# Attention, MLP and gated MLP in one kernel: the first attention block reordered, and its side work moved

## The chip, the cores and the metric

The kernel runs on one core of one Trainium2 chip, as one program. The metric is the device time of one execution in microseconds (us). The engines are named as the profile names them: PE is TensorE's matrix multiply, PEld its weight load, DVE is VectorE, ACT is ScalarE, POOL is GpSimd, SP is SyncE, which here only issues DMAs. "PEq", "SPq" and so on are the instruction queues of these engines.

## What is computed

Three layers follow one another: decayed causal attention, a normalised MLP with a residual, and a second MLP whose gate mixes the positions of a sequence.

```python
# attention: B=4, H=8, S=576, D=64
scores = (1/sqrt(D)) * q @ k.T
cum    = cumsum(log(clip(f, 1e-4, 1)))
scores = where(causal, -1e9, scores + cum[:, None] - cum[None, :])
x      = softmax(scores) @ v                      # heads side by side: 512 wide
# first MLP, 512 -> 2048 -> 512
xn = (x - mean(x)) / sqrt(var(x) + 1e-6) * g_ln
x  = x + relu(xn @ w_ch1) @ w_ch2
# second MLP
h  = relu(x @ w_in); u, v = h[:, :512], h[:, 512:]
vs = einsum("ts,bsd->btd", w_spatial, norm(v)) + b_spatial
out = (u * vs) @ w_out
```

## The kernel before

The 2304 positions are cut into nine blocks of 256 columns (the list `BLOCKS`, line 43). A block holds two batches times 128 queries, or one batch times 256 queries; blocks 0 and 1 are the first 128 positions of batches 0, 1 and of batches 2, 3. `attention32` (L324) computes these two in float32, four pairs of heads each; `attention1` computes blocks 2 and 3, and `attention` the rest. For each pair `attention32` does four score matmuls (L356; the decay comes in as two extra rows of the operands, 64 and 65), mask and row minimum on DVE (L359), the exponential with its sum on ACT (L361), 1/sum (L364, L365), a diagonal matrix of 1/sum on DVE (L369), four matmuls that transpose and scale (L373), a copy out of PSUM on ACT (L374, the tile `PT`), four matmuls with v (L381) and a copy of the result into `xT` on ACT (L382). In L381 the second head of a pair uses 128 columns of v and writes all 128 rows of PSUM, then the first head uses 64 columns and overwrites the upper half.

When the four pairs of a block are there, `norm` (L614) makes the mean over the 512 channels (L622, L611), subtracts it (L625, "centre"), squares (L628), adds on POOL (L632, L633), makes the mean of the squares (L611), and from it 1/sqrt, the tile `y` (L636 to L640). For the first block `y` is not applied to the input of the MLP; it is applied at the very end of the group (L738), since relu lets a positive factor through.

The first MLP runs over eight groups of blocks; group 0 is block 0, group 1 is block 1. A group walks over 16 slices j of the hidden width: `ph(j)` is x times a slice of w_ch1 (L708, 8 instructions in float32), a relu on ACT (L715), and two steps later `acc` gets the slice of w_ch2 (L693). The weights come in as 64-bit floats, 1 MB for a slice: `load_raw` (L539) issues the DMAs, `narrow` (L518) makes 32-bit floats of them with two passes on ACT (L531, L532) and three on DVE (L533 to L535). `PACE` and `LOWAT` (L58, L59) say behind which event the ACT passes of the first slices may stand; the marks are `done[i]` (i counts PT copies of block 0, then relus) and "split" (the last copy of the scaled input of group 0, L672). Group 0 runs in float32 while the weights arrive. `squares(j)` (L561) multiplies each weight slice with itself on PE (L569) to get the weights' norms; `scales` (L575) sums them and derives power-of-two scales (the matmul L588 is the mark "sums"); `make16(j)` (L593) then splits each slice into two 16-bit halves in place (ACT L598, DVE L601). Groups 1 to 7 run on these halves. `SUMS = 13` keeps ph(13) and what is behind it in group 0 back until "sums", as work for PE during the change from group 0 to group 1. `vnorm` (L228) does the same as `squares` for v: five loads of 1 MB and 80 matmuls (L246), needed by block 3 and later.

At the start `decays` (L146) computes the cumulative logarithm on DVE and ACT; the decay rows of block 0 go from SBUF to SBUF by DMA (L343). `gscale` (L188) loads the norm's weights g_ln broadcast over 128 partitions and derives a scale; it is used from group 1 on. `WARM = 54` dummy matmuls (L1039) run on PE while the first loads arrive.

The program text gives each step a place on a common time line (`SPAN`, `BEGIN`, `CONV`, `MAKE`, `VN`, L48 to L62, and the list of events in `run`). A planner then orders the instructions of each engine by this order and by its own estimate of when each is ready; `after` (L123) adds an order between two instructions without a semaphore. Each engine and each DMA queue works its list strictly in that order. Pools of SBUF tiles have a fixed number of buffers (`BUFS0` for blocks 0 and 1), and a PSUM bank has a tag: `acc` and `ph` have two banks, `s2` two, `s` and `av` one each.

## Time and profile before

| | us |
|---|---|
| median of 3 runs | 790.46 (790.35 to 790.98) |
| the profiled execution | 790.74 |
| its span, first to last instruction | 789.0 |
| PE busy | 765.5 (97%) |
| DVE busy | 549.5 (70%) |
| ACT busy | 520.5 (66%) |
| POOL busy | 60.3 (8%) |
| mean granted TensorE clock | 0.989 |

A busy time on PE is the time between the start of a matmul and its modelled end; dummy matmuls count, and so do matmuls at half clock. The page's slices show where PE is idle or slow; the table of windows gives PE, DVE, ACT and the granted clock of any stretch; the list of waits says for whom an engine waited; the timeline gives the instructions in the order of time. Seven eighths of the span are groups 1 to 7 and the second MLP, which the change does not touch.

### The profile page before, as it was taken

How to read it: one execution, taken by the hardware profiler on the slowest of the kernel's cores; microseconds unless marked ns; L12 is line 12 of the kernel's file. 1: busy time of each engine (PE TensorE's matmuls, PEld its weight loads, DVE VectorE, ACT ScalarE, POOL GpSimd, SP SyncE). 2: the span in 40 equal slices, each digit the busy share in tenths (PEclk: the TensorE clock that was granted, in tenths of full speed). 3: DMA queues.
4: the chain of work that ended last, by engine and by line, in shares of the span. 5: the costliest groups of instructions: out<-in, count | busy, mean ns of one | idle time of the engine just before them, and what ended most of it. 6: DMA issues, size and time to landing. Idle time of an engine off the chain costs nothing.

```text
span 789.0 us, 16305 instructions
## 1 busy us (share of the span) xinstructions
PE 765.5 (97%) x5978; PEld 581.9 (74%) x5978; DVE 549.5 (70%) x1490; ACT 520.5 (66%) x1315; POOL 60.3 (8%) x89
## 2 busy tenths in 40 slices
PE   8799999999999999999999999999998999999998
PEld 7488887887877877788888888544446667668676
DVE  5699589849389889979858855687526662654634
ACT  5787489839388889888858844485417633656543
POOL 4100011011011001110201100100021000000000
PEclk8989999999999999999999999999999999999999
DMA  8888576278679998996995955731043230000101
GB/s 255 220 305 292 188 210 104 55 145 125 142 208 165 189 242 151 204 220 140 195 186 120 125 88 172 198 111 50 1 78 50 80 109 1 31 31 7 57 1 61
DMA packets 164228, 104.72 MB, mean 133 GB/s; under 512 B 106179, under 2 KB 151363, under 8 KB 164149
## 3 DMA queue, kind: packets, MB, share of 16 engines
q1 hardware_dynamic: 157848, 96.63, 50.9%
q0 software_dynamic: 5296, 5.28, 5.3%
q10 hardware_dynamic: 1004, 1.78, 0.8%
q8 instruction: 47, 0.77, 0.4%
q14 instruction: 33, 0.26, 0.1%
HBM read 64.37 MB, written 15.11 MB: 101 GB/s over the span
## 4 chain that ended last, share of the span: by engine, by line
PE 58%; DVE 13%; issue 12%; ACT 7%; DMA 7%; POOL 1%; SPq 1%; DVEq 0%; ACTq 0%; POOLq 0%
PE ph L708 13%; PE acc L693 12%; PE pb L648 7%; PE pb L649 7%; PE pb L650 7%; PE av L460 3%; PE s L296 3%; DVE P L317 2%; DMA PT<-P 2%; DVE wt L601 2%; DMA vr<-in_v_dram 2%; DMA qk<-in_qk_dram 1%; DVE sd L300 1%; PE gram L569 1%; PE av L381 1%
## 5 line engine op out<-in xcount | busy, mean ns | idle before, releaser
L693 PE MATMUL acc<-hh,wt 128*128 128x256 f16 (+2 forms) x960 | 198.5, 296 | 0.8 <-DVE t L736 0.5
L708 PE MATMUL ph<-xh,wt 128*128 128x256 f16 (+1 forms) x896 | 187.3, 289 | 5.6 <-DVE hl L719 5.2
L708 PEld LDWEIGHTS <-wt 128*128 128x128 f16 x1344 | 127.1, 98 | 52.0 <-issue 13.7
L693 PEld LDWEIGHTS <-wt 128*128 128x128 f16 x1344 | 129.2, 98 | 44.1 <-issue 5.2
L708 PE MATMUL ph<-xl,wt 128*128 128x256 f16 (+1 forms) x448 | 129.3, 289 | 0.0
L693 PE MATMUL acc<-hl,wt 128*128 128x256 f16 (+1 forms) x416 | 115.9, 282 | 0.3 <-DVE hl L719 0.3
L715 ACT ACTIVATE hh<-ph 128x256 f16<-128x256 f32 (+2 forms) x128 | 51.0, 399 | 60.4 <-PE ph L708 60.2
L719 DVE SCALAR_TENSOR_TENSOR hl<-ph,hh 128x256 f16<-128x256 f32 (+1 forms) x112 | 50.5, 453 | 40.1 <-ACT hh L715 39.6
L261 ACT ACTIVATE P<-sd,st 128x512 f16<-128x512 f32 (+1 forms) x128 | 70.5, 586 | 9.6 <-DVE st L307 7.9
L317 DVE SCALAR_TENSOR_TENSOR P<-sd,st,P 128x384 f16<-128x384 f32 (+1 forms) x96 | 58.6, 633 | 9.3 <-ACT P L261 8.8
L304 ACT ACTIVATE sd<-sd,st 128x384 f32<-128x384 f32 (+2 forms) x80 | 54.6, 683 | 15.2 <-DVE st L300 15.0
L296 PE MATMUL s<-x 68*128 68x384 f32 (+7 forms) x256 | 63.3, 360 | 0.1
L300 DVE CUSTOM_DVE_ANT_0 sd<-s,mask 128x384 f32<-128x384 f32 (+2 forms) x80 | 45.8, 579 | 3.9 <-PE s L296 2.8
L740 POOL DMA_DIRECT2D x_d<-t x36 | 32.3, 1081 | 188.4 <-DVE t L736 149.3
L261 ACT ACTIVATE x<-qk 64x320 fp32r<-64x320 f32 (+1 forms) x64 | 41.4, 699 | 1.0 <-DMA qk<-in_qk_dram 1.0
L991 DVE SCALAR_TENSOR_TENSOR u<-pb,wsc,u 128x288 f32<-128x288 f32 x32 | 15.9, 514 | 34.3 <-PE pb L990 34.3
L296 PEld LDWEIGHTS s<-x 68*128 68x128 f32 (+3 forms) x256 | 36.9, 178 | 2.4 <-issue 0.9
L648 PE MATMUL pb<-wsh,vl 128*128 128x288 f16 x128 | 36.6, 286 | 1.3 <-ACT u L934 1.1
L649 PE MATMUL pb<-x2l,wih 128*128 128x288 f16 (+2 forms) x144 | 37.8, 273 | 0.0
L648 PE MATMUL pb<-x2h,wil 128*128 128x288 f16 (+2 forms) x144 | 37.8, 273 | 0.0
L650 PE MATMUL pb<-x2h,wih 128*128 128x288 f16 (+2 forms) x144 | 37.8, 273 | 0.0
L650 PE MATMUL pb<-wsh,vh 128*128 128x288 f16 x128 | 36.6, 286 | 0.0
(281 smaller groups left out, 1596.8 us busy)
## 6 DMA issues: line engine op xcount, KB each, us to landing
raw<-in_moe_w_ch_dram SPq DMA_DIRECT2D x32, 512.0 KB
qk<-in_qk_dram SPq DMA_DIRECT2D x32, 448.0 KB
vraw<-in_v_dram SPq DMA_DIRECT2D x5, 1024.0 KB
vr<-in_v_dram SPq DMA_DIRECT2D x16, 320.0 KB
x_d<-xT SPq DMA_DIRECT2D x9, 512.0 KB
x_d<-t POOLq DMA_DIRECT2D x36, 128.0 KB, 4.4
out_dram<-o SPq DMA_DIRECT2D x32, 144.0 KB
raw<-in_moe_w_in_dram SPq DMA_DIRECT2D x8, 512.0 KB
```

Source lines behind the costliest of these rows:

```text
L261: self.nc.scalar.activation(out, in_, AF.Copy, scale=scale)
L296: nc.tensor.matmul(ps[: R * u + R, : c1 - c0], lhsT=x[:, lo - q0 - R * u : hi - q0], rhs=y[:, c0:c1], start=g == 0, stop=g == len(heads[u] ...
L300: nc.vector.tensor_tensor_reduce(out=sd[:M, c0:c1], in0=ps[:M, : c1 - c0], in1=mask, scale=-0.125, scalar=3e38 if n == 0 else st[:M, n - 1 ...
L304: nc.scalar.activation(sd[:M, :N], sd[:M, :N], AF.Exp, bias=st[:M, n : n + 1], scale=-1.0, accum_out=st[:M, 2:3])
L317: low = nc.vector.scalar_tensor_tensor(out=dl, in0=src, scalar=rs, in1=dh, op0=ALU.mult, op1=ALU.subtract)
L648: first = mm(out, lhsT=al, rhs=bh, start=start, stop=False, **kw)
L649: mm(out, lhsT=ah, rhs=bl, start=False, stop=False, **kw)
L650: mm(out, lhsT=ah, rhs=bh, start=False, stop=stop, **kw)
L693: ins = nc.tensor.matmul(acc[m], lhsT=a, rhs=b, start=bank not in clear, stop=last and e == len(terms) - 1, skip_group_check=True)
L708: ins = nc.tensor.matmul(ph, lhsT=a, rhs=b, start=k == e == 0, stop=k == NK - 1 and e == len(terms) - 1)
L715: relu = nc.scalar.activation(hh, ph, AF.Relu)
L719: nc.vector.scalar_tensor_tensor(out=hl, in0=ph, scalar=0.0, in1=hh, op0=ALU.max, op1=ALU.subtract)
```

## The change

- **Block 0 only: all scores first.** The four pairs' scores, minimum, exponential and 1/sum come ahead of all transposes and products with v. The tile `e` gets a fourth buffer; the scores of pairs 2 and 3 go to the `s2` banks.
- **Fills.** `WARM` falls from 54 to 34 dummy matmuls; new dummy matmuls of the same kind (`fill`, 256 columns in bf16) stand behind the scores of pairs 1 and 3 (4 each), behind the transposes of each pair (4) and behind its products with v (3): 36 in all.
- **Loads of block 0.** The two decay rows are issued from two queues, SP and ACT, behind two pairs of q and k; v comes behind all four pairs. Both DMAs of the first weight slice now stand behind these loads (before, only the first of the two did).
- **v zero-padded.** `vm` holds v of each head with zeros in the other head's 64 columns. Two memsets on DVE and, for each block, two copies on POOL. The products with v now all have 128 columns, and the second head adds to the first.
- **Work moved from ACT and POOL in `decays`.** The negated decay rows go from ACT to POOL, two memsets from POOL to DVE.
- **Deferred.** The second step of block 0's norm (from L628 on) and `gscale` come at 0.1 of group 0, `gscale` on POOL's DMA queue and behind "split". Two copies on ACT into `mask4` come behind "split".
- **First weights earlier.** The first ACT pass of slice 1 stands behind "x3", the copy L382 of pair 3, and no longer behind "split"; its DVE passes stand behind "centre". The second ACT pass of slices 1 and 2 stands behind "x3" and "split".
- **Squares, scales, vnorm.** `squares(j)` stands behind ph(j) (from slice 9 on one slice ahead); the sums are taken behind ph(14), and `SUMS` is 15, so that only ph(15) is kept back. The matmuls of `vnorm` stand behind ph(0) of group 1. Block 1's first scores stand behind the first squares.

```diff
-BUFS0 = dict(vr=1, qk=1, e=3, diag=2, PT=2, st=4)
+BUFS0 = dict(vr=1, qk=1, e=4, diag=2, PT=2, st=4)
-WARM = 54
+WARM, FILLS = 34, (4, 4, 3)
-PACE = (1, "split", "split", "split", "split")
-LOWAT = (1, 2, 3)
-SUMS = 13
+PACE = (1, "x3", "split", "split", "split")
+LOWAT = (1, "x3", "split")
+SUMS = 15
+REST = 0.1
+BESIDE = 9
-WSC, MAKE, VN = 0.63, 0.64, 0.7
+WSC, MAKE, VN = 0.875, 0.876, 1.01
...
+        for e, t, r, w in ((nc.gpsimd, decay, 1, P), (nc.vector, f32(dec), 2, S), (nc.gpsimd, dec1, 1, P)):
+            e.memset(t[:, :r, w:], 1.0)
+            e.memset(t[:, r:, :w], 1.0)
...
-        nc.scalar.activation(dec[:, 2, S:], f32(h), AF.Copy, scale=-1.0)
-        nc.scalar.activation(dec[:, 3, S:], f32(l), AF.Copy, scale=-1.0)
+        for r, x in ((2, h), (3, l)):
+            nc.gpsimd.tensor_scalar(out=dec[:, r, S:], in0=f32(x), scalar1=-1.0, scalar2=1.0, op0=ALU.mult, op1=ALU.mult)
...
-        nc.scalar.dma_start(out=g, in_=self.moe_g_ln.rearrange("p k -> (p k)").partition_broadcast(P))
+        nc.gpsimd.dma_start(out=g, in_=self.moe_g_ln.rearrange("p k -> (p k)").partition_broadcast(P))
...
+    def fill(self, n, behind=None):
+        ones = self.ones.bitcast(BF16)
+        for i in range(n):
+            ins = self.nc.tensor.matmul(self.warm[:, : 2 * P], lhsT=ones[:, :P], rhs=ones, start=True, stop=True)
+            if behind is not None:
+                self.after(ins, behind)
+                behind = None
...
+        if not b:
+            self.vm = at.tile([P, 2, NP, 2, P], F32, name="vm")
+            for u in range(2):
+                clear = nc.vector.memset(self.vm[:, :, :, u, 64 - 64 * u : P - 64 * u], 0.0)
+                self.after(clear, self.scan)
...
-                    loads.append(nc.sync.dma_start(out=row, in_=self.decay[b * H : (b + 2) * H, r]))
-                loads.append(nc.sync.dma_start(out=vra, in_=self.v[b : b + 2, :P].rearrange("b p d -> p b d")))
+                    queue = nc.scalar if r and not b else nc.sync
+                    loads.append(queue.dma_start(out=row, in_=self.decay[b * H : (b + 2) * H, r]))
+        loads.append(nc.sync.dma_start(out=vra, in_=self.v[b : b + 2, :P].rearrange("b p d -> p b d")))
+        for u in range(2):
+            us = slice(64 * u, 64 * u + 64)
+            v = vra.rearrange("p n (q w) -> p n q w", w=P)
+            nc.gpsimd.tensor_copy(out=vm[:, :, :, u, us], in_=v[:, :, :, us])
...
+            elif p == 0:
+                for i in range(NP):
+                    ahead.append(scores(i))
+                    yield
...
-            for n in range(2):
-
-                for u in (1, 0):
-                    mm(pav[: 64 * u + 64, 0, n], lhsT=vr[:, n, : 64 * u + 64], rhs=pt[:, n, u], start=True, stop=True, skip_group_check=True)
+            for n, u, c in four_:
+                ins = mm(pav[:, 0, n], lhsT=vm[:, n, p, u], rhs=pt[:, n, u], start=u == 0, stop=u == 1, skip_group_check=True)
...
-        nc.sync.dma_start(out=raw[:, DM:], in_=self.moe_w_ch2[cs, :])
+        second = nc.sync.dma_start(out=raw[:, DM:], in_=self.moe_w_ch2[cs, :])
+        if j == 0:
+            self.after(second, self.marks["loads"])
...
+            if g == 0:
+                self.marks["hidden"] = ins
+                if j < BESIDE:
+                    self.squares(j)
+                if BESIDE <= j + 1 < NF:
+                    self.squares(j + 1)
...
+            if n == 0:
+                with self.tc.high_priority(1):
+                    next(g)
+                self.rest = g
+                return xc
```

## Rows read from the trace of the kernel before

**Rows 1.** Windows: from:to, length, busy us (instructions) by engine, granted clock, DMA share, GB/s.

```profile
14.00:21.00 7.00, 6.97 (x31) 6.16 (x29) 4.16 (x22) 4.95 (x26) 0.00 (x0) 0.51 1.07 384
...
34.00:38.00 4.00, 2.35 (x9) 1.08 (x7) 1.41 (x2) 4.00 (x6) 2.00 (x2) 0.98 0.44 144
38.00:45.00 7.00, 5.88 (x22) 4.89 (x22) 6.60 (x9) 6.66 (x18) 0.00 (x0) 0.52 0.91 315
45.00:100.00 55.00, 55.00 (x366) 47.38 (x365) 42.86 (x75) 35.24 (x67) 0.00 (x0) 1.00 0.71 250
```

**Rows 2.** Waits of PE, 0 to 62 us: for whom, total us, times, longest.

```profile
PE gram L569 <- DVE wt L535: 1.1, 1, 1.1
```

**Rows 3.** Timeline to 34 us: start, length, engine, line, operation, count, idle before.

```profile
0.81 0.92 SPq L154 DMA_DIRECT2D ft<-in_f_dram  x1
...
3.19 0.61 SPq L546 DMA_DIRECT2D raw<-in_moe_w_ch_dram  x1
3.57 0.52 DVE L168 TENSOR_SCALAR ft<-ft 32x128 f32<-32x128 f32 x2 [2.35 <-DMA ft<-in_f_dram]
...
5.26 1.23 SPq L343 DMA_DIRECT2D qk<-decay  x2
...
10.14 2.05 PE L356 MATMUL acc<-qk 66*128 66x128 f32 x16
...
13.17 3.39 PE L356 MATMUL acc<-qk 66*128 66x128 f32 x16 [0.98 <-DMA qk<-in_qk_dram]
...
30.45 0.38 ACT L382 ACTIVATE xT<-s 128x256 f32<-128x256 f32 x1 [0.71 <-PE s L381]
...
33.40 1.56 PE L708 MATMUL ph<-xg,wt 128*128 128x256 f32 x6 [1.25 <-ACT xg L672]
```

**Rows 4.** Chain of waits, 0 to 140 us: start, us, engine, line, instructions.

```profile
67.42 0.46 PE gram L569 x8
...
69.66 1.36 PE av L381 x8
...
76.14 1.73 PE ph L708 x8
...
80.53 0.89 PE s L373 x8
```

**Rows 5.** Lines 361, 374 and 531 to 100 us: ns min/median/max, starts.

```profile
L361 ACT ACTIVATE e<-e,st x32: 385/388/422, 11.8 to 84.1; 128x128 f32<-128x128 f32 x32
...
L374 ACT ACTIVATE PT<-ph x4: 575/597/599, 18.6 to 28.1; 128x512 f32<-128x512 f32 x4
...
L531 ACT ACTIVATE wt<-raw x16: 1118/1149/1173, 21.5 to 89.9; 128x1024 f32<-128x1024 f32 x16
```

**Rows 6.** Lines 693 and 708, from the sums to group 1: ns, starts.

```profile
L693 PE MATMUL acc<-hh,wt x45: 379/379/462, 100.5 to 124.1; 128*128 128x256 f32 x45
...
L708 PE MATMUL ph<-xg,wt x24: 379/379/462, 101.8 to 116.5; 128*128 128x256 f32 x24
```

**Rows 7.** Timeline of the change from group 0 to group 1.

```profile
100.75 0.28 PE L588 MATMUL gram<-gss,ones 128*128 128x2 f32 x2
...
119.67 1.71 ACT L669 ACTIVATE xh<-xT,gs 128x256 f16<-128x256 f32 x4 [1.47 <-DVE xT L642]
...
125.26 0.27 PE L708 MATMUL ph<-xh,wt 128*128 128x256 f16 x1
```

**Rows 8.** Windows around the start of group 1, columns as above.

```profile
101.00:125.00 24.00, 24.00 (x179) 20.98 (x179) 22.21 (x65) 20.63 (x53) 2.39 (x3) 1.00 0.82 199
...
130.00:137.00 7.00, 5.79 (x31) 4.03 (x31) 7.00 (x25) 7.00 (x19) 0.00 (x0) 0.76 0.35 82
```

**Rows 9.** Timeline, 108 to 112 us: DVE and POOL side by side.

```profile
108.24 0.75 DVE L601 SCALAR_TENSOR_TENSOR wt<-wt,w2c 128x512 f16<-128x512 f32 x1
...
108.95 1.27 POOL L632 TENSOR_TENSOR sq<-sq 128x512 f32<-128x512 f32 x1 [71.70 <-ACT sq L628]
...
109.66 1.12 DVE L601 SCALAR_TENSOR_TENSOR wt<-wt,w1c 128x512 f16<-128x512 f32 x1
```

More of the change, by code (lines that the diff above doesn't have):

```diff
@@ L349, in attention32, with scores @@
         yield
-        for p in range(NP):
-            qk, vr = qka[:, p], vra[:, :, p * P : (p + 1) * P]
-            ps, e, diag = bank(tags[0]), four("e"), four("diag")
+        def scores(p):
+            qk = qka[:, p]
+            ps, e = bank("s2" if p > 1 else tags[0]), four("e")
             st = at.tile([P, 2, 4], F32, tag="st", name="st", bufs=bufs["st"])
-            four_ = [(n, u, 2 * n + u) for n in range(2) for u in range(2)]
             for n, u, c in four_:
-                mm(ps[:, n, u], lhsT=qk[:, u, n, :P], rhs=qk[:, u, n, P:], start=True, stop=True, skip_group_check=True)
+                ins = mm(ps[:, n, u], lhsT=qk[:, u, n, :P], rhs=qk[:, u, n, P:], start=True, stop=True, skip_group_check=True)
+                if b and p == c == 0:
+                    self.after(ins, self.first)
+            if not b and p % 2:
+                self.fill(FILLS[0], ins)
             for n, u, c in four_:
@@ L365, in attention32 @@
             nc.vector.reciprocal(st[:, 1], st[:, 1])
[L366 to L368 removed]
+            return e, st
+        four_ = [(n, u, 2 * n + u) for n in range(2) for u in range(2)]
+        ahead = []
+        for p in range(NP):
+            if b:
+                ahead.append(scores(p))
+                yield
+            elif p == 0:
+                for i in range(NP):
+                    ahead.append(scores(i))
+                    yield
+            e, st = ahead[p]
+            ps, pt, diag = bank(tags[1]), four("PT"), four("diag")
             nc.vector.tensor_tensor(
@@ L515, in tail, with narrow @@
         return d[:, c : c + n].rearrange("(k p) t -> p k t", p=P)
-    def narrow(self, raw, tmp, low=None):
+    def narrow(self, raw, tmp, low=None, behind=None):
         nc = self.nc
@@ L558, in load_w @@
         if j < len(LOWAT):
-            self.after(self.low, self.done[LOWAT[j]])
+            self.after(self.low, self.marks[LOWAT[j]] if isinstance(LOWAT[j], str) else self.done[LOWAT[j]])
     def squares(self, j):
@@ L1036, in run @@
         self.at = at_cm.__enter__()
-        warm, ones = self.bank("s2"), self.ones.bitcast(BF16)
-        for i in range(WARM):
-            self.nc.tensor.matmul(warm[:, : 2 * P], lhsT=ones[:, :P], rhs=ones, start=True, stop=True)
+        self.warm = self.bank("s")
+        self.fill(WARM)
         with self.pool("dk") as dk:
@@ L1123, in run @@
             elif kind == -1:
-                if n < NF:
+                if n < 0:
+                    drain(self.rest)
+                    self.gscale()
+                elif n < NF:
                     self.load_w(n)
                     converted = n + 1
-                    if n >= len(CONV):
-                        for i in range(n + 1) if n == len(CONV) else [n]:
-                            self.squares(i)
                 elif n == NF:
```

50 lines of the change are left out of this document (30 added, 20 removed).

## The prediction

> **What bounds the kernel now.** I first read the windows, to see where PE is idle or slow, since PE is busy for 97% of the span and the rest of the kernel cannot move unless PE's work starts earlier or gets less. From 45 to 100 us PE is busy in all of the 55 us at the full clock, while DVE is busy for 42.9 and ACT for 35.2 us [rows 1]: here PE is the bound, and the other two have slack of 12 and 20 us. The front is different. The first MLP matmul stands at 33.40 us [rows 3]; PE's work before it is the attention of block 0, which is a chain, and dummies. After it PE is idle for 1.65 us from 34 to 38 and for 1.12 us from 38 to 45, and from 38 to 45 it has about half the clock (1.2 instead of 2.4 GHz), so that 5.88 us of busy time do about 3.0 us of full-speed work [rows 1]. So the front loses 33.4 us to the chain and then 2.8 + 2.9 = 5.7 us. The second place is the start of group 1 at 125.26 us [rows 7]: from 130 to 137 PE is idle for 1.2 us and has a granted clock of 0.76, which costs 7 x 0.24 = 1.7 us, while DVE and ACT are busy all the time [rows 8]. These two places are what the change touches; everything behind them I take as PE-bound and moved as a whole.
>
> Next I read the timeline of the front. The decay rows are issued at 5.26 us, as the cumulative sum is ready, and the first scores run at 10.14 us; the scores of pairs 2 and 3 wait for q and k until 13.17 us; the last result of block 0 is copied from 30.45 to 30.83 us [rows 3].
>
> **The change, step by step.** The sum goes against the profiled execution: 790.74 us, of which the span is 789.0; the median of the runs is 0.28 us lower, which I leave out of account.
>
> *First scores.* A DMA into an empty queue, that of f, takes from 0.81 to 3.57 us, 2.76 us from issue to landing; the decay rows take from 5.26 to 10.14 us, 4.88 us, though they are small, as 512 KB of raw weights were issued at 3.19 us ahead of them, with g_ln's broadcast [rows 3]. Both move behind. By the 2.76 us the first scores stand at 8.0 us: 2.1 us earlier. The second row on ACT's queue saves one of two issues, half of 1.23 us [rows 3], which is in these 2.1. Bounds: 0.6 (only that issue) to 2.7. Moved past SP's queue is v: it lands behind all four pairs, and its first reader is the product of pair 0, which waits for a PT copy anyway. The two DVE memsets fit into the 2.35 us in which DVE waits for f [rows 3].
>
> *Body of block 0.* From the first scores to the last copy it takes 30.83 - 10.14 = 20.7 us [rows 3]. New: ACT begins 1.7 us after the first scores, as now (11.8, [rows 5], against 10.14), at 9.7 us. Sixteen exponentials at 0.39 us [rows 5] take 6.2 us and the four small copies between them at most as much as one each, to 16 to 17.5 us; PT copies cannot go earlier, if the planner keeps to program order. I take 16.4. By then PE has done all scores and two transposes. What is left is a chain of PT copy (0.6 us, [rows 5]), transposes, PT copy, products, copy, on PE four times the products, twice the transposes, at 0.89 us per four matmuls [rows 4] = 5.3 us, some 17 fills ahead of the last product, and the last copy of 0.38 us [rows 3]. A fill lies between an instruction of the transposes, 0.89 / 8 = 0.11 us, and one of ph, 1.73 / 8 = 0.22 us [rows 4]; nearer to the first, as it is one pass in 16 bits: 17 x 0.11 = 1.9 us. With 0.9 us for the steps between the engines: 16.4 + 0.6 + 5.3 + 1.9 + 0.4 + 0.9 = 25.5 us for the end of the last copy, a body of 17.5 us: a gain of 3.2. Bounds: 5.2 (fills and transposes hide behind ACT) and -0.2 (a stretch at half clock like that from 14 to 21 us, clock 0.51 [rows 1], which costs 7 x 0.49 = 3.4 us, comes back, though the fills are there).
>
> *From the last copy to the MLP.* 30.83 to 33.40 us, 2.6 us of sum, mean, subtraction and scaling [rows 3], is unchanged in itself: the first MLP matmul stands at 28.1 us. The wait for "x3" now lets two ACT passes of slice 1 start, 1.15 us each [rows 5]; behind them on ACT stand the scaled inputs, ready some 2 us after "x3", so that they may come 0.3 us late. That is part of the next bound.
>
> *The gap behind it.* PE waits there for slice 1, which DVE narrows late (1.1 us, [rows 2]), as its ACT pass stands behind "split", and for the squares and means of the norm. The ACT pass now stands behind "x3", 2.6 us earlier, and the norm's second step is gone to 0.1 of the group, where DVE and ACT have slack. I leave about 1.3 us of idle time and 1.7 us for half a stretch at low clock, as PE still has holes between the last product and slice 1: 3.0 instead of 5.7, a gain of 2.7. Bounds: 0.5 (the low clock stays in full and only the norm's mean drops out) to 4.7 (1 us is left).
>
> *Products with v.* Four matmuls with 128 and 64 columns in turn take 1.36 us, those of the transposes, as many and as large, 0.89 us [rows 4]. With 128 columns throughout I price them at 0.89. In block 1, which runs where PE is full, this gives 4 x 0.47 = 1.9 us; block 0's share is in its body. Bounds: 0 to 1.9, as no row shows the padded form; the transposes are nearest in shape and type. The POOL copies of v lie beside the exponentials; behind them on POOL stands nothing that block 0 reads, and the products wait for them.
>
> *POOL's copies against DVE.* A POOL addition of 512 columns takes 1.27 us, and the DVE instruction beside it 1.12 us instead of 0.75 [rows 9]. Two copies in block 0 may meet the diagonals on DVE: 0.4 us, bounds 0 to 1.5. The Trainium skill ("SBUF — State Buffer", "Who interferes with whom") says that a DVE instruction with two SBUF inputs and a GpSimd one that reads SBUF exclude each other for the whole instruction. By that rule two copies would cost up to 2.5 us, and the sum would be 2.1 us higher; the row shows a stretch of 0.37 us, not of 1.27.
>
> *Squares and the handover to group 1.* The squares cost PE the same wherever they stand. But the sums now follow ph(14). In the old order 45 + 24 instructions of group 0 are behind the sums [rows 6], which at 1.73 us for 8 [rows 4] are 14.9 us; now ph(15) and three steps of `acc` are, 32 instructions, 6.9 us. And the 80 matmuls of `vnorm`, as large as those of the squares (0.46 us for 8, [rows 4]), 4.6 us, go behind group 1's ph(0). So PE has 12.6 us less to fill the handover, which took 100.75 to 125.26 us, 24.5 us [rows 7]. What must happen in it is less than that: the sums, the scales and one `make16` (about 3 us), and the scaled input of block 1, made at 119.67 us [rows 7] behind five `make16` and block 2's first steps on full DVE and ACT queues (22.2 and 20.6 of 24 us, [rows 8]). Block 1 itself ends earlier with the front, and in the new order the sums come later relative to it, so its norm can go first. I price the handover at no change: its cover is 6.9 us of group 0 and the scores of block 2. Bounds: -2.9 (the idle and low-clock time behind 130 us goes) to +3.
>
> *At nothing.* The deferred `gscale`, the copies into `mask4` and the negated decay rows on POOL lie beside PE's full stretch or are read much later, by block 2 on; if the cover were gone, these ten short instructions, at no more than an exponential's 0.39 us [rows 5], would cost up to 3.9 us.
>
> Sum: 2.1 + 3.2 + 2.7 + 1.9 - 0.4 = 9.5 us; 790.7 - 9.5 = **781.2 us**.
>
> **The rivals.**
>
> *PE paces block 0.* Scores, transposes and products at 0.89 to 1.0 us each make 11 us, 36 fills 4 us or more: nearly as much as the body itself. With one stretch at half clock it grows by 3.4 us: 784.6. For it: the clock fell at 14 us after PE had waited for 0.98 us [rows 3], and 20 fewer warming matmuls leave a hole before the scores.
>
> *The new order does not come out.* The planner places each instruction by its own estimate; if the narrowing of slice 0 or late exponentials stand between the PT copies, the body keeps its 20.7 us and 2.1 + 2.7 + 1.9 - 0.4 = 6.3 us are left: 784.4, and with the gap at its lower bound 786.6. I take 785.5.
>
> *The handover is freed.* If DVE and ACT have worked off block 2's first steps before the sums, the 2.9 us go too: 778.3.
>
> *POOL excludes DVE.* If a diagonal waits for a whole copy, two copies of 1.27 us [rows 9] stand in the way instead of 0.4 us: 783.3. This is the rule quoted above.
>
> *Slower: the handover starves PE.* The front hands 9.5 us to group 0, but 14.9 - 6.9 = 8.0 us more of group 0 stand ahead of the sums, so these come at about 99.3 us, 1.5 us earlier only. If DVE and ACT still need 24.5 us from there, group 1 starts at 123.8 us, PE has stood idle for a good 10 us, the 4.6 us of `vnorm` follow on PE's path, and a low clock after the idle time costs another 1.7 us: -1.5 + 4.6 + 1.7 = +4.8, 795.5 us. It ends slower from a handover of 20 us on. Against it: block 1 ends earlier, and most of the 22.2 us of DVE are not needed for group 1's first step.
>
> **How the numbers follow.** The forecast has 0.50, PE pacing block 0 0.15, the order not coming out 0.12, the freed handover 0.08, POOL's exclusion 0.05, the starved handover 0.10. The range of 8 in 10 takes in the unknown costs of the front, of which the bounds won't all fall on one side, and all rivals but the slower one: 775.5 to 788.0. A measurement can tell 0.2%, 1.6 us, from no change. Slower by that: 0.09; within: 0.04, from the worst ends of the second and the slower rival; faster: 0.87.
>
> **What would show it.** The first scores at about 8 us; sixteen exponentials in one run on ACT; the copy of pair 3 at about 25 us; the first MLP matmul at about 28 us, and less than 1.5 us of idle time behind it; 0.9 us for the products of a pair; the sums near 99 us and group 1's first matmul by 110 us. Wrong would be: a last copy later than 28 us, a clock of 0.5 after 28 us for as long as before, or PE idle by several us between the sums and group 1.

## The result and the profile after

The changed kernel takes 800.5 us (median of 4 runs, 798.2 to 803.4) against 790.4 us for the kernel before (790.2 to 791.0) on the same chip: a ratio of 1.013, 95% interval 1.009 to 1.016. It is slower by 10 us where 781.2 us was predicted. The profiled execution took 801.2 us with a span of 799.5 us, 10.5 us more than that of before (789.0).

I read the two traces by four marks that every kernel here has: the first MLP matmul of group 0, the first matmul of group 1 (`ph` of 16-bit halves), and the moments at which POOL issues the first store `x_d` of each group. The differences between marks say in which stretch time is won or lost:

| stretch, us | before | after | difference |
|---|---|---|---|
| start to first MLP matmul | 33.40 | 29.98 | -3.4 |
| to group 1's first matmul | 91.86 | 93.71 | +1.9 |
| to group 1's store | 68.87 | 73.77 | +4.9 |
| to group 2's store | 56.57 | 57.24 | +0.7 |
| to group 4's store | 131.73 | 137.60 | +5.9 |
| to the end of the span | 406.57 | 407.20 | +0.6 |

The stores of groups 1, 2 and 4 (start, length, engine, line, operation, count, idle before), first of the kernel before, then of after:

```profile
194.13 2.67 POOL L740 DMA_DIRECT2D x_d<-t  x3 [18.84 <-DVE t L736]
...
250.70 2.69 POOL L740 DMA_DIRECT2D x_d<-t  x3 [7.34 <-DVE st L307]
...
382.43 2.68 POOL L740 DMA_DIRECT2D x_d<-t  x3 [5.50 <-DVE t L736]
```

```profile
197.46 2.63 POOL L798 DMA_DIRECT2D x_d<-t  x3 [21.64 <-DVE t L794]
...
254.70 2.65 POOL L798 DMA_DIRECT2D x_d<-t  x3 [9.52 <-DVE t L794]
...
392.30 2.67 POOL L798 DMA_DIRECT2D x_d<-t  x3 [6.64 <-DVE t L794]
```

The front wins 3.4 us. Up to group 1's store twice as much (6.8 us) is lost again, and another 5.9 us are lost between the stores of groups 2 and 4 (254.7 to 392.3 us), in whose program text nothing was changed.

The timeline of the front after (start, length, engine, line, operation, count, idle before):

```profile
2.74 0.74 POOL L196 DMA_DIRECT2D gall<-in_moe_g_ln_dram  x1
...
5.18 0.59 SPq L362 DMA_DIRECT2D qk<-decay  x1
...
9.09 2.02 PE L379 MATMUL acc<-qk 66*128 66x128 f32 x16 [2.01 <-DMA qk<-decay]
...
10.71 0.40 ACT L388 ACTIVATE e<-e,st 128x128 f32<-128x128 f32 x1 [3.59 <-DVE st L386]
...
16.68 0.39 ACT L388 ACTIVATE e<-e,st 128x128 f32<-128x128 f32 x1
...
27.12 0.38 ACT L423 ACTIVATE xT<-s 128x256 f32<-128x256 f32 x1 [1.27 <-PE s L420]
...
29.98 1.99 PE L758 MATMUL ph<-xg,wt 128*128 128x256 f32 x8 [1.27 <-ACT xg L722]
...
34.71 1.56 PE L758 MATMUL ph<-xg,wt 128*128 128x256 f32 x6 [1.32 <-DVE wt L577]
```

Beside [rows 3]: the first scores stand at 9.09 us instead of 10.14, all sixteen exponentials run without a break from 10.71 us on, the last copy ends at 27.50 instead of 30.83, and the gap behind the first MLP matmul is down to the wait of 1.32 us for DVE. The front does what the change says but for one load: g_ln's broadcast (`gall`) is still issued at 2.74 us, ahead of the decay rows. Only its use is deferred, not the load, though the description of the change and the forecast have both behind. Windows after (columns as in rows 1), to be read beside [rows 1] and [rows 8]:

```profile
14.00:21.00 7.00, 5.66 (x36) 5.36 (x37) 3.61 (x12) 5.47 (x22) 0.00 (x0) 0.76 1.04 386
34.00:38.00 4.00, 3.29 (x21) 2.89 (x22) 4.00 (x13) 3.88 (x10) 3.18 (x2) 1.00 0.71 253
38.00:45.00 7.00, 6.73 (x37) 5.57 (x36) 6.61 (x12) 5.66 (x14) 0.00 (x0) 1.00 0.80 249
60.00:80.00 20.00, 18.34 (x125) 16.25 (x124) 17.66 (x29) 15.09 (x26) 0.00 (x0) 1.00 0.86 294
100.00:120.00 20.00, 14.76 (x86) 12.72 (x84) 16.19 (x57) 16.64 (x46) 2.14 (x2) 0.95 0.36 93
120.00:140.00 20.00, 14.26 (x101) 10.57 (x102) 17.62 (x49) 17.76 (x44) 3.58 (x4) 0.71 0.51 92
```

The same two last windows of the kernel before:

```profile
100.00:120.00 20.00, 20.00 (x140) 17.48 (x140) 17.21 (x52) 16.01 (x41) 2.33 (x2) 1.00 0.82 226
120.00:140.00 20.00, 18.79 (x158) 15.22 (x159) 20.00 (x57) 19.84 (x51) 3.58 (x4) 0.91 0.59 91
```

From 100 to 140 us PE was busy for 38.8 of 40 us; now it is busy for 29.0, and from 120 on with a mean granted clock of 0.71. What PE waited for, 98 to 150 us (engine, line, waited for, total us, times, longest), and its timeline in that place:

```profile
PE av L474 <- DMA PT<-P: 3.8, 2, 3.2
PE av L474 <- DVE t L688: 2.9, 1, 2.9
PE ph L758 <- ACT xh L719: 1.8, 1, 1.8
```

```profile
107.02 0.28 PE L637 MATMUL gram<-gss,ones 128*128 128x2 f32 x2
107.16 1.97 PE L758 MATMUL ph<-xg,wt 128*128 128x256 f32 x8
...
111.54 1.99 PE L743 MATMUL acc<-hh,wt 128*128 128x256 f32 x8 [0.77 <-ACT hh L773]
...
117.33 0.53 PE L474 MATMUL av<-PT,vp 128*64 128x128 f16 x12 [2.93 <-DVE t L688]
...
123.69 0.58 PE L758 MATMUL ph<-xh,wt 128*128 128x256 f16 x2 [1.80 <-ACT xh L719]
```

The sums (107.02) come 6.3 us later than before [rows 7], and behind them PE has 16 matmuls of group 0 left, ph(15) and one step of `acc`, and after 113.5 us only block 2 and waits until group 1 begins at 123.69 us. Before, the matmuls of `vnorm` lay there as well. Windows of `vnorm`'s instructions alone (length, busy us and count of PE, PEld and DVE, clock, DMA share, GB/s), first of the kernel before, then of after:

```profile
100.00:120.00 20.00, 4.22 (x57) 0.00 (x0) 0.00 (x0) 1.00 0.82 226
120.00:140.00 20.00, 1.97 (x26) 0.30 (x2) 0.83 (x2) 0.91 0.59 91
```

```profile
150.00:160.00 10.00, 1.88 (x31) 0.00 (x0) 0.00 (x0) 1.00 0.46 89
160.00:170.00 10.00, 2.92 (x43) 0.00 (x0) 0.00 (x0) 1.00 0.97 277
170.00:180.00 10.00, 0.92 (x14) 0.30 (x2) 0.85 (x2) 1.00 0.58 157
```

`vnorm` filled 6.2 us of the handover; now it has none there, and its 5.7 us stand between 150 and 180 us, where PE is full anyway (busy for 29.5 of 30 us).

### The profile page after: what moved, and what is told of

Its sections match the earlier page's. It is cut to its first block, busy times and chain, and to the rows that moved or that the text cites. A ratio compares the mean times of both kernels' runs of the same rounds, so it can differ in the third digit from the quotient of the medians.

```text
span 799.5 us, 16351 instructions
## 1 busy us (share of the span) xinstructions
PE 759.0 (95%) x5994; PEld 581.8 (73%) x5994; DVE 553.9 (69%) x1494; ACT 521.8 (65%) x1313; POOL 63.6 (8%) x94
## 4 chain that ended last, share of the span: by engine, by line
PE 59%; DVE 12%; issue 12%; DMA 9%; ACT 7%; POOL 1%; SPq 0%; ACTq 0%; DVEq 0%; POOLq 0%
PE acc L743 13%; PE ph L758 12%; PE pb L698 7%; PE pb L699 7%; PE pb L700 7%; PE s L299 4%; PE av L502 3%; DMA PT<-P 3%; DMA raw<-in_moe_w_ch_dram 2%; DVE P L320 1%; DMA vr<-in_v_dram 1%; ACT x L264 1%; DMA vraw<-in_v_dram 1%; DVE low L576 1%; ACT sd L307 1%
## 5 line engine op out<-in xcount | busy, mean ns | idle before, releaser
L758 PEld LDWEIGHTS <-wt 128*128 128x128 f16 x1344 | 128.1, 99 | 52.8 <-issue 14.7
L299 PE MATMUL s<-x 68*128 68x384 f32 (+7 forms) x256 | 61.7, 357 | 2.0 <-DVE x L282 0.8
```

What stands on the lines that cost most here:

```text
L299: nc.tensor.matmul(ps[: R * u + R, : c1 - c0], lhsT=x[:, lo - q0 - R * u : hi - q0], rhs=y[:, c0:c1], start=g == 0, stop=g == len(heads[u] ...
L758: ins = nc.tensor.matmul(ph, lhsT=a, rhs=b, start=k == e == 0, stop=k == NK - 1 and e == len(terms) - 1)
```

## The experiments

Single executions of these runs spread by some 4 us to either side (the kernel before: 787 to 796), so whole times are given with the interval of their ratio. Each kernel has one trace, so a stretch of a single kernel shows little by itself, and stretches are compared over several kernels. Two theories: **A**, the handover from group 0 to group 1 costs the 10 us that the front doesn't; **B**, part of the loss is that the planner orders the untouched later groups differently (against it A', that the later loss hangs on the handover too). The planned lists of SP's queue bear on B: from block 4 on they are the same, entry by entry, in the changed kernel and in the front-only kernel, and the same in the kernel before and in that with the handover alone (run 2). I call these two the order of after and the order of before.

**1. The front alone.** The changed kernel with the old handover; the squares are back at the events that load the weights, and the order of vnorm behind ph(0) is out. The change also draws the events of the five `make16` and of `vnorm` closer together (steps of 0.001 and 0.015 instead of 0.02 and 0.05); this run takes that back too, and run 2 has it.

```diff
-SUMS = 15
+SUMS = 13
-WSC, MAKE, VN = 0.875, 0.876, 1.01
+WSC, MAKE, VN = 0.63, 0.64, 0.7
...
-                    self.after(ins, self.marks["entered"])
```

> The changed kernel with the handover of before: the sums behind ph(13), scales and make16 at 0.63 and 0.64 of group 0, the norm's sums of w (vnorm) from 0.7 on, the squares where they were. The new front stays: all scores first, the decay rows on two queues, zero-padded v, the deferred second step. Theory A (the handover costs some 8 us, and the later stretch from 325 to 392 us some 8 us more, which belongs to the new front, since the queue order of SP's transposes and loads in the later groups is that of the changed kernel here too): first x_d store of group 0 about 120, of group 1 about 189, of group 3 about 318, of group 4 about 385, and 790 to 793 us in all. Theory A' (all of the loss hangs on the handover, the later stretch too): 785 us, with group 4 stored at about 377. If the front itself is what costs, group 0's store stands no earlier than 123 and the time is 795 or more.

791.8 us, ratio 1.003 (1.001 to 1.006). Group 0 is stored at 118.33 us, group 1 at 188.08: 6.1 us earlier than before, while group 4 (382.50) is where it was. As A foretold, but for group 3, stored at 313.55 and not at about 318; A' is out.

**2. The handover alone**, on the kernel before, with vnorm behind group 1's ph(0) and squares(j) behind ph(j).

```diff
-SUMS = 13
+SUMS = 15
+BESIDE = 9
-WSC, MAKE, VN = 0.63, 0.64, 0.7
+WSC, MAKE, VN = 0.875, 0.876, 1.01
...
+                    self.after(ins, self.marks["entered"])
```

> The kernel before, with the new handover alone: sums behind ph(15), squares behind ph, scales and make16 at 0.875, vnorm behind group 1's ph(0). Front and products with v as before. Theory A: from group 0's x_d store (124.9) to group 1's it takes 77.4 us as in the changed kernel, and not 69.2, so +8 at group 1; the queue order of the later groups is that of before, so nothing more is lost after it: 798 us. Theory A' (the later loss belongs to the handover): 806 us. If the handover costs only because the front ended early: no change, 790 to 791 us.

799.4 us, ratio 1.013 (1.011 to 1.015): the handover alone is as slow as the whole change. Group 1 is stored at 202.55, 8.4 us later than before; the sums stand at 110.95. From 95 to 105 us DVE and ACT have next to nothing to do, where in the front-only kernel they are full. First this kernel, then the front-only one:

```profile
95.00:105.00 10.00, 10.00 (x60) 8.28 (x59) 0.70 (x2) 0.80 (x3) 0.00 (x0) 1.00 0.34 99
```

```profile
95.00:105.00 10.00, 10.00 (x72) 8.81 (x71) 9.77 (x20) 9.70 (x24) 1.52 (x2) 1.00 0.81 240
```

**3. make16 of slices 1 to 4 later.** Those of the slices behind them move back by four places as well.

```diff
-SOON = 5
+SOON = 1
```

> The changed kernel, but make16 of slices 1 to 4 comes in group 1's first half and not ahead of its first scaled input. Theory C (the handover is long because make16 and block 2's steps stand ahead of block 1's norm on DVE and ACT): group 1's first ph 3 to 5 us earlier than 123.7, and the time 3 us or more below the changed kernel's 800.5. Theory D (the sums come too late, and PE has no work left to cover the norm, whoever stands ahead): within 1.5 us of 800.5.

796.4 us, ratio 1.007 (1.003 to 1.011). Group 1's first matmul stands at 115.13 us, 8.6 earlier than in the changed kernel (1.3 of them from the start of the MLP), and group 1's store 5.9 earlier. So the five `make16` ahead of block 1's scaled input do delay it once the sums are late (with early sums this was not tried); group 1 itself then takes longer (76.4 us to its store).

**4. vnorm early again, sums late.**

```diff
-WSC, MAKE, VN = 0.875, 0.876, 1.01
+WSC, MAKE, VN = 0.875, 0.876, 0.89
...
-                    self.after(ins, self.marks["entered"])
```

> The changed kernel, but the 80 matmuls of vnorm may run as soon as the scales are made, ahead of group 1's ph(0), where PE waits. If vnorm costs its 4.6 us on PE's path behind ph(0): 796 us. If the wait of PE for the transposes of block 2 and for the norm sets the end anyway, or vnorm's operands are late too: within 1.5 us of 800.5.

805.6 us, ratio 1.020 (1.016 to 1.023): both expectations missed, it got worse. The last two loads of v go out as late as 113.8 and 114.8 us, and PE now waits for loads of v in the middle of the handover (98 to 150 us):

```profile
PE vgram L248 <- DMA vraw<-in_v_dram: 4.2, 2, 3.0
```

Group 1's first matmul stands at 129.50 us, and its store comes 78.1 us later, though `vnorm` no longer stands in that stretch (changed kernel: 73.8). With late sums, then, vnorm does better behind ph(0); that is no gain against early sums.

**5. One dummy more before the kernel.** Nothing but this, on the kernel before:

```diff
-WARM = 54
+WARM = 55
```

> The kernel before with one dummy matmul more in its warming run (55 instead of 54), nothing else. Theory B: what costs 7 to 9 us between the stores of groups 3 and 4 is the order that the planner gives to the later groups, and it depends on the smallest shift of the front; with this one matmul SP's queue of the later groups comes out in the order of the changed kernel. Then the interval from group 3's x_d store to group 4's is 67 to 69 us and not 59, and the time 797 to 799. If the front's work itself (other data in flight, the deferred second step) causes the later loss: 790.5 to 791 us.

798.0 us, ratio 1.006 (1.003 to 1.008). The interval from group 3's store to group 4's is 67.15 us, as B foretold, but group 2 to 3 takes 3.8 us less than before, so that the two together cost 4.2 us; another 2.4 us are lost ahead of group 1's store.

**6. The front alone, one fill more in each place**, which brings the order of before back:

```diff
-WARM, FILLS = 34, (4, 4, 3)
+WARM, FILLS = 34, (5, 5, 4)
```

> The front-only kernel with one more fill matmul in each place (5, 5, 4 instead of 4, 4, 3). More work by 11 dummies, but SP's queue of the later groups comes out in the order of before. Theory B: groups 3 to 4 take 59 to 60 us again, and the front's gain of 6 to 9 us stays to the end: 782 to 784 us. Otherwise as the front-only kernel: 791 to 793.

790.6 us, ratio 0.998 (0.996 to 1.001). Group 3 to 4 takes 60.3 us, as expected; but group 2 to 3 takes 75.2 instead of 69.6, and the gain is not there at the end. The expected 782 to 784 us were missed.

**7. The changed kernel with 3 fills each**, the order of before again:

```diff
-WARM, FILLS = 34, (4, 4, 3)
+WARM, FILLS = 34, (3, 3, 3)
```

> The changed kernel with 3, 3, 3 fills instead of 4, 4, 3; its later queue order is that of before. Theory B with A: the later loss goes, the handover's 8 us stay: group 0 to 1 takes 77 us, group 3 to 4 60 us, 792 to 794 us in all. If the later loss hangs on the handover: 800.

793.7 us, ratio 1.002 (0.999 to 1.004). Group 0 to 1 takes 77.9 us, group 3 to 4 60.2 us, as expected: the handover's loss stays and the later one shrinks, without any change to the handover. Six fills less (one behind the transposes of each pair, one behind the scores of pairs 1 and 3) bring the ratio from 1.013 to 1.002.

**8. vnorm behind group 1's ph(0), sums early**, on the kernel before:

```diff
-WSC, MAKE, VN = 0.63, 0.64, 0.7
+WSC, MAKE, VN = 0.63, 0.64, 1.01
...
+                    self.after(ins, self.marks["entered"])
```

> The kernel before, but vnorm's 80 matmuls stand behind group 1's ph(0); sums, scales and make16 as before (sums behind ph(13)). If the missing cover of vnorm's 4.6 us and their place on PE's path is what makes the handover long: group 0's store to group 1's 4 to 5 us longer than the 69.2 of before. If the late sums are (scales and block 2 wait for them, and DVE and ACT idle until then): within 1.5 us of 69.2. The order of the later groups is a third one here, so the whole time says little.

791.5 us, ratio 0.999 (0.996 to 1.002). Group 0 to 1 takes 74.4 us, 5.2 more than before, about the 4 to 5 of the first case. Group 1's first matmul comes at 121.0 us, 4.2 earlier than before, and its store 3.7 later. Another, shorter order of the later groups (130.5 us from group 2 to 4) gives that back.

**9. The front alone with fills 2, 2, 2**, yet another order:

```diff
-WARM, FILLS = 34, (4, 4, 3)
+WARM, FILLS = 34, (2, 2, 2)
```

> The front-only kernel (new front, old handover) with fills 2, 2, 2 instead of 4, 4, 3. SP's queue in the later groups is a third order, neither that of before nor that of the changed kernel. Theory B (the order decides): from group 1's store to the end not the 600.2 us of the front-only kernel but another figure, which I can't foretell; group 1's store at 188 to 190. If fills matter for the front, group 0's store lies 2 us or more later than the 118.3 of the front-only kernel, with a lower clock in block 0.

785.5 us, ratio 0.994 (0.992 to 0.996): faster than the kernel before and than the changed one. Group 1 is stored at 184.76, earlier than I had expected, group 2 to 4 takes 130.5 us. The clock is at 0.50 from 14 to 21 us (run 1: 1.00) and the first MLP matmul stands at 32.01 us, 1.6 us later than in run 1; group 0's store lies 1.1 us later, not 2 or more.

**10. Sums two steps earlier, vnorm still late.**

```diff
-SUMS = 15
+SUMS = 13
-WSC, MAKE, VN = 0.875, 0.876, 1.01
+WSC, MAKE, VN = 0.70, 0.701, 1.01
...
-                if j < BESIDE:
-                    self.squares(j)
-                if BESIDE <= j + 1 < NF:
-                    self.squares(j + 1)
+                for i in [j] if j < 8 else [2 * j - 8, 2 * j - 7]:
+                    if i < NF:
+                        self.squares(i)
```

> The changed kernel with the squares of two slices per step from ph(8) on, so that the sums stand behind ph(12) and not behind ph(14); the scales and make16 follow at 0.70. vnorm stays behind group 1's ph(0). Theory A1 (the lateness of the sums keeps DVE and ACT idle until 107 us, and leaves PE too little of group 0): DVE and ACT are busier before 105 us, group 1's store at 192 to 194 and not 197.5, 3 to 5 us earlier. Theory A2 (all that counts is vnorm behind ph(0)): group 1's store within 1.5 us of 197.5. The later groups have another order here, so it's read from group 1's store.

792.7 us, ratio 1.004 (1.002 to 1.006). The sums come at 92.31 us, 14.7 us earlier than in the changed kernel and earlier even than before. Group 1's first matmul comes 3.8 us and its store 4.7 us earlier than in the changed kernel (1.2 of them from the start of the MLP): A1's figure. A good half of the handover's loss stays with the late vnorm.

**11. The front alone without fills**, the order of before:

```diff
-WARM, FILLS = 34, (4, 4, 3)
+WARM, FILLS = 34, (0, 0, 0)
```

> The front-only kernel without any fills; SP's queue in the later groups is that of before. If the fills hold the clock up in block 0: from 14 to 28 us the granted clock is lower than in the front-only kernel (as in the kernel before, 0.51 from 14 to 21), and the first MLP matmul stands 1.5 to 3 us later than its 30.4. If they only take PE's time, it stands 1 us earlier or the same. Theory B: from group 1's store to the end 595 to 600 us, as with the other kernels that have the order of before (594.9 to 600.2).

786.3 us, ratio 0.995 (0.992 to 0.997). The clock in block 0 is at its lower level from 14 to 21 us (0.50, where run 1 has 1.00), yet the first MLP matmul stands at 29.82 us, 0.6 earlier than in run 1 (30.43). With the fills the clock is up, but they buy no time: they stand on PE's path themselves (see the body of block 0 below). Group 1's store to the end takes 596.3 us, within what B expected.

**12. Ten warming matmuls less**, on the kernel before, the order of before:

```diff
-WARM = 54
+WARM = 44
```

> The kernel before with 44 instead of 54 warming matmuls: a larger change of the warming run than that with 55, but SP's queue of the later groups stays as before. Theory B: no change, 790 to 792 us, and from group 3's store to group 4's 59 to 61 us. If it is the number of warming matmuls that counts and not the order: 795 or more, as with 55.

794.9 us, ratio 1.005 (1.003 to 1.008), where B had 790 to 792 and the other case 795 or more. The later groups take 61.7 us (expected 59 to 61), but the first MLP matmul stands at 37.51 us, 4.1 later than before. SP's list is that of before from end to end; DVE's is not: the diagonal of pair 3 stands behind a further narrowing pass and two sums. First the kernel before, then this one, where PE waits 1.8 us for it:

```profile
26.14 0.69 DVE L369 TENSOR_TENSOR diag<-ident,st 128x512 f32<-128x512 f32 x1
```

```profile
28.81 0.68 DVE L369 TENSOR_TENSOR diag<-ident,st 128x512 f32<-128x512 f32 x1
```

The clock is lower too (0.50 from 34 to 38 us, before 0.98). How the 4.1 us divide between order and clock no run shows.

**13. One warming matmul less**, the order of after:

```diff
-WARM = 54
+WARM = 53
```

> The kernel before with 53 instead of 54 warming matmuls. SP's queue of the later groups comes out in the order of the changed kernel, as with 55. Theory B: group 3's store to group 4's 66 to 69 us, group 2's to group 3's 69 to 71, together 135 to 139 against the 131.7 of before, and 794 to 798 us in all. If the loss with 55 came from the front of that run: 790 to 792.

800.8 us, ratio 1.012 (1.009 to 1.014): one dummy matmul less costs as much as the whole change, and more than the 794 to 798 us that B gave. Group 3 to 4 takes 66.0 us, but with group 2 to 3 it is 134.6, just under the 135 to 139 expected: only 2.9 us are lost there; 4.8 us are lost between groups 1 and 2 and 2.7 in the handover.

**14. The front alone with vnorm behind ph(0)**, sums early, the order of after:

```diff
-WSC, MAKE, VN = 0.63, 0.64, 0.7
+WSC, MAKE, VN = 0.63, 0.64, 1.01
...
+                    self.after(ins, self.marks["entered"])
```

> The front-only kernel, but vnorm's 80 matmuls stand behind group 1's ph(0); sums and squares as before. The later queue order is the same as in the front-only kernel and in the changed kernel. From the first MLP matmul to group 1's store the front-only kernel takes 157.7 us, the changed kernel 167.5. If both the late sums and the late vnorm cost: 161 to 164, and 795 to 797 us in all. If it is vnorm alone: 166 to 168, 799 to 801. If it is the sums alone: 157 to 159, 791 to 793.

795.5 us, ratio 1.005 (1.002 to 1.008). By the whole time it is the first case (both cost), by the stretch from the MLP's start to group 1's store (167.7 us) the second. The finer marks show where: group 1's first matmul stands at 119.03 us, as in run 1 (118.56): with early sums it isn't delayed. Its store comes 79.3 us later, where run 1 takes 69.5.

Windows of the front-only kernel (run 1), then of this one, show PE without that work, busy for 16.4 us instead of 18.4 and at a lower clock:

```profile
120.00:140.00 20.00, 18.36 (x158) 15.06 (x157) 20.00 (x57) 18.76 (x50) 1.90 (x3) 0.91 0.48 86
```

```profile
120.00:140.00 20.00, 16.43 (x118) 12.77 (x119) 18.22 (x52) 18.84 (x51) 3.58 (x4) 0.74 0.53 93
```

**The handover, over all kernels.** From the first MLP matmul to group 1's store, the four kernels with the new front and the old handover (runs 1, 6, 9, 11) take 152.8 to 159.5 us, 157.1 on average; the two with the new front and the new handover (after, run 7) take 167.5 and 166.5. With the old front it is 158.6 to 163.4 us, 161.4 on average, with the old handover (before, runs 5, 12, 13), and 169.3 with the new one (run 2). The ranges don't meet: the new handover as a whole costs some 8 to 10 us.

How this divides between the late sums and the late `vnorm` is less sure. From the first MLP matmul to group 1's first one, the five kernels with the new front and early sums (runs 1, 6, 9, 11, 14) take 87.4 to 89.4 us; the changed kernel and run 7, with late sums, 93.7 and 92.2, some 4.5 us more, and in run 3 (86.4), where four of the five `make16` no longer stand ahead of block 1's input, that cost is gone. On the old front run 2's 94.7 us lie within what kernels with early sums take (86.8 in run 8, 91.9 before, 96.7 in run 13). From group 1's first matmul to its store, the eight kernels with early sums and the early vnorm take 65.4 to 73.7 us, 69.0 on average (before, runs 1, 5, 6, 9, 11, 12, 13), and the seven with vnorm behind ph(0) 72.9 to 79.3, 75.4 on average (after, runs 2, 3, 7, 8, 10, 14): 6.4 us, against 5.7 to 6.7 us of PE time of vnorm itself. But run 4, with late sums and the early vnorm, takes 78.1. And over both stretches together the two fronts disagree: the late vnorm alone costs 2.2 us on the old front (run 8, 163.6) and 10.6 on the new one (run 14, 167.7); late sums on top of it cost 5.7 us on the old front (run 2) and nothing on the new one (after, run 7). One trace of each kernel, each with a planned order of its own in this stretch, can't settle that.

**The later order.** From group 2's store to group 4's, the six kernels with the order of before (before, runs 2, 6, 7, 11, 12) take 131.7 to 135.5 us, 133.4 on average; the seven with the order of after (after, runs 1, 3, 4, 5, 13, 14) 134.6 to 138.5, 136.3 on average. So B holds for 3 us on average and 5.9 in the changed kernel. Only the two intervals together can be read: between the stores of groups 3 and 4 PE has 562 to 567 instructions in the order of after and 539 to 541 in that of before, so part of what moves from one interval to the other is the same work on the other side of the mark. PE's waits from run 1, group 3's store to group 4's, then from the kernel before, and one window of run 1:

```profile
PE av L501 <- DMA PT<-P: 2.7, 1, 2.7
PE acc L740 <- ACT hh L766: 2.0, 2, 1.6
```

```profile
PE av L460 <- ACT hh L715: 0.5, 1, 0.5
PE acc L693 <- DVE t L736: 0.5, 1, 0.5
```

```profile
330.00:340.00 10.00, 7.30 (x54) 5.01 (x52) 5.81 (x16) 5.29 (x15) 0.20 (x1) 0.72 1.02 178
```

In the order of after PE stands for one block's transposed probabilities and for a relu, and then runs at a lower clock for a while. The wait for the relu (1.3 to 2.0 us) and the lower clock (0.95 to 0.98 from group 3's store to group 4's) are there in all seven kernels with that order, the wait for the probabilities in five. Which entry of the queues is to blame was not tried, since the planner's order can't be set entry by entry.

## Why the prediction was wrong, step by step

*What bounds the kernel* (the two places, the front and the handover) was right. "Everything behind them I take as PE-bound and moved as a whole" was wrong: 5.9 of the 10.5 us were lost there. Runs 5 and 13 show how little that assumption holds in this kernel: one dummy matmul at the front moves the end by 6 and by 9 us, and in both the planner has the untouched groups in another order.

*First scores.* Predicted 8.0 us, measured 9.09: a gain of 1.05 instead of 2.1. The decay rows were issued at 5.18 us, much as before, and PE waited for them until 9.05: 3.9 us on two queues that hold no weights ahead of them any more, not the 2.76 of f's transfer. The step was wrong in two ways. It let g_ln's broadcast "move behind", but its load was issued ahead of the rows, at 2.74 us, and landed at 8.10. And it took an empty queue for empty DMA engines: from 5 to 7 us these were full. More than half of that was the broadcast, which is all that POOL had issued by then (queue q0); q1 has the loads that SP issued. The two queues in this window, after (packets, MB, share of the time of the 16 engines):

```profile
q0 software_dynamic: 80, 0.26, 55.3%
q1 hardware_dynamic: 193, 0.17, 46.2%
```

The bound of 0.6 was nearer than the term.

*Body of block 0.* 18.4 us (9.09 to 27.50) instead of 17.5, before 20.7: 2.3 of the 3.2 us. The exponentials came out in one run, so the second rival fell. The rival that PE paces the block was right for its second half, though not in its price: from 15.34 us to the last copy the chain of waits holds nothing but PE, with 25 fills at 3.2 us (the step has 17 at 1.9), and ACT waits for PE. The chain, after (start, us, engine, line, instructions):

```profile
15.34 1.92 PE ph L412 x8
17.25 0.85 PE s L331 x4
...
26.19 0.91 PE s L420 x8
```

What the block lacks is the clock. Up to 100 us run 3 does the same instructions in the same order on every engine; its clock is at 1.00 from 14 to 21 us, where the changed kernel has 0.76. Its transposes of the first two pairs take 1.13 us each instead of 1.92 and 1.54, its body takes 17.2 us, and its first MLP matmul stands 1.3 us earlier. Run 3:

```profile
14.00:21.00 7.00, 5.53 (x48) 5.20 (x48) 4.68 (x13) 6.58 (x24) 0.10 (x1) 1.00 1.04 392
```

```profile
28.71 1.99 PE L758 MATMUL ph<-xg,wt 128*128 128x256 f32 x8 [1.27 <-ACT xg L722]
```

So part of the low clock came back "though the fills are there", as the step's lower bound has it.

*Last copy to MLP.* 2.5 us (27.50 to 29.98) against 2.6. Right.

*The gap behind it.* It loses 1.3 us in the wait for the narrowing of slice 1, ahead of which gscale's reduction takes 0.6 us of the chain on DVE (the step "At nothing" has it beside PE's full stretch), and 0.3 from 38 to 45 us, and the clock stays at its upper level: better than the 3.0 us predicted. But PE waits for 1.66 us from 60 to 80 us in block 1, where it had waited for nothing [rows 1], all in one wait of the products for the PT copy on ACT. So of the expected 2.7 us about 2.4 are there net (5.7 - 1.6 - 1.7).

*Products with v.* 0.89 us for a pair, as predicted, shown by the chain of waits of after in block 1 (start, us, engine, line, instructions), where the clock is full; one of the three there is at 1.16:

```profile
70.45 1.16 PE av L420 x8
...
86.18 0.89 PE av L420 x8
```

*POOL against DVE.* The two copies of v for block 1 took 2.60 us and DVE's pass beside them 1.63 us instead of 1.23; in block 0, where no pass of that kind stood beside the copies, they took 1.17. Timeline of POOL and of DVE, after:

```profile
12.71 1.17 POOL L367 COPY vm<-vr 128x512 f32<-128x512 f32 x2 [2.35 <-DMA vr<-in_v_dram]
30.19 2.60 POOL L367 COPY vm<-vr 128x512 f32<-128x512 f32 x2 [16.31 <-DMA vr<-in_v_dram]
```

```profile
30.69 1.63 DVE L576 SCALAR_TENSOR_TENSOR low<-raw,low 128x1024 uint32<-128x1024 uint32 x1
```

DVE lost the 0.4 us of the sum, though not at block 0's diagonals, the first of which stands at 14.50 us, behind the copies. POOL lost 1.4 us, and nobody waited for it. The Trainium skill ("SBUF — State Buffer", "Who interferes with whom") lets a DVE instruction with two SBUF inputs and a GpSimd one that reads SBUF exclude each other. The trace agrees for the slowed pass: the first copy ends at 31.25 us, 0.56 us after the start of the pass, and the pass ends 1.07 us behind that copy; the second copy, begun at 31.19 us, ends at 32.79, 0.47 us behind the pass. That fits each waiting for the rest of the other's instruction, and the 0.4 us are such a rest. POOL lost 0.45 of its 1.4 us already in the first copy, beside the DVE pass ahead, which has one input.

*The handover.* This is **the step that failed**: "I price the handover at no change: its cover is 6.9 us of group 0 and the scores of block 2". Alone it makes the kernel before slower by 1.3% (run 2), and over all kernels it costs 8 to 10 us up to group 1's store. Three of its premises were wrong. The sums came at 107.0 us and not at 99.3: the `acc` of the earlier steps ran ahead of them, so that 16 matmuls, not 32, were left behind. What they release was not short: with the sums late, DVE and ACT first idle (DVE is busy for 0.4 us from 90 to 100 us) and then have `make16`, block 1's norm and block 2 at once, and block 1's input is ready at 123 us. And I wrote down myself that PE would have 4.6 us of `vnorm` less to fill the stretch, and then priced this at nothing: the step moves 6 us of filler from a place where it kept PE busy to one where PE is full. What each of the three costs by itself stays open (for `vnorm` 2.2 us on one front and 10.6 on the other). The slower rival had the starved handover and the 4.6 us of `vnorm` on PE's path. That its 123.8 us for group 1 is what was measured (123.69) is luck: it took the sums at 99.3 us and 24.5 us from there, and they were 107.0 and 16.7. I gave it 0.10, since "most of the 22.2 us of DVE are not needed for group 1's first step", which run 3 shows to be no argument: they stand ahead of it in the queue. It named 795.5 us; the 5.9 us of the later order are not in it.

*The sum.* At group 1's store the front alone (run 1) is 6.1 us ahead of before, run 11 5.7, where the same terms, the products among them, had 9.5. At the end the front is worth 0.5 to 0.6% in runs 9 and 11 (785.5 and 786.3 us), nothing that can be told in run 6, and it costs 0.3% in run 1: 0.25% of gain on average, where 1.2% was forecast. Runs 6 and 11 differ in fills alone and have the same order on DVE, POOL and SP from end to end, so the order is not all that decides it.

## What to carry to other kernels

Work that fills a stretch in which the main engine waits for others is not free to move: moved to a place where that engine is full, it can cost its whole length or more (here 2.2 and 10.6 us for 6 us of work), so price it by where it goes, not by its being the same work. A step that releases much other work (here the sums) costs by what queues up behind it on the other engines, so look at what stands there before holding it back. A dummy put in to keep the clock up stands on the engine's path like any other instruction. And where a planner orders the whole program from estimates, compare a change with a few variants that differ in a dummy instruction before crediting or blaming it for less than 1%; here one dummy was worth up to 1.2%.

## What the runs showed of the hardware

The lower clock cost 1.3 us in the new block 0: with the same instructions in the same order, the first MLP matmul stands at 29.98 us with a clock of 0.76 from 14 to 21 us (after) and at 28.71 us with 1.00 (run 3). What put the clock at one level or the other in these two executions no run shows. Without fills (run 11) the clock was at 0.50 there and the first MLP matmul at 29.82 us, with 20 of the 36 (run 9) at 0.50 and 32.01 us, with all of them (run 1) at 1.00 and 30.43 us. In none of the three does PE wait in the second half of the block, so that the fills of run 1 cost there about what its clock gives back. In the old block 0, run 12's loss of 4.1 us went with a lower clock and with another order on DVE. The decay rows, small as they are, took 3.9 us from issue to use, 1.1 us more than f, with f, q, k and g_ln's broadcast issued ahead of them: a second queue did not help them while the DMA engines behind both were busy (shares of 1.04 in all from 5 to 7 us). Which of the loads held them up, no run separates.
